# Gating weight loads, shortening the lag between two layers, and moving transposes to DMA in an attention + two-layer kernel

## The chip, the cores and the metric

One core of one Trainium2 chip. The metric is device microseconds of one execution, as the median of several; a "profile" is one traced execution, and its span is about 1.8 us shorter than the timed value of the same execution. Every ratio below is the mean time of one kernel's fast runs over the mean of the kernel before's fast runs in the same rounds, so it is not quite the ratio of the medians that are quoted beside it. Chips differ by about a per cent, so kernels are compared on one chip, or by these ratios. A run more than 1.5% above the fastest of its kernel is called slow and left out of the ratios; the medians quoted are of all runs.

## The reference

Eight batches; each has eight heads of 512 rows `x` and 32 rows `state`, 64 wide. Both attend to each other, and all rows go through a two-layer block.

```python
scores  = x @ state.T / 8 ;  a  = softmax(scores)  ; xread = a  @ state      # 512 rows a batch
scores2 = state @ x.T / 8 ;  a2 = softmax(scores2) ; sread = a2 @ x          # 32 rows a batch
rows = concat([xread, sread])           # heads side by side: (8 * 544) x 512
h = rows @ w_in                         # 512 -> 2048
g = s * relu(h) ** 2 + b
out = g @ w_out                         # 2048 -> 512, float32
```

## The kernel before

It folds `state @ w_in` into a matrix M for each batch, so that layer 1 of the 512 x rows is `a @ M`. Work is cut into slots. Batch `s` has 16 slots; slot `f` computes one 128-row block of the hidden layer, `h_f` (two matmuls of 512 columns), its relu on ScalarE and its square on VectorE, then a piece of the attention of a later batch (`todo`), then one "layer-2 slot" (four matmuls of 512 columns) of hidden blocks computed `LAG` slots earlier. I call the 16 slots of batch 0 "stage 0", those of batch 1 "stage 1", and so on. The order on TensorE is the program's; the other engines are ordered by a scheduler.

```python
# loads: x[0] and the first states on the hardware queues, all else from gpsimd, at once
nc.scalar.dma_start(stf[:, 0:NG, :], st_v[:, 0:NG, :])
nc.scalar.dma_start(ident16, ident_dr.ap())
for i in range(4):
    nc.sync.dma_start(xf[:, 2 * i : 2 * i + 2], x0_v[:, 2 * i : 2 * i + 2])
# ... cut: constants, casts of x[0] and state to fp16 ...
load_wi(0); load_wi(1); load_x(1); load_wi(2); load_wi(3)     # 512 KB fp16 each, cast from 1 MB fp32
for q in range(4): load_wo(q)
load_x(2)  # ... cut: the remaining states, x[3] to x[7] ...

def att_xT(b, i):             # transposes of x on TensorE, through PSUM
    ps = att_ps([P, 4, 2, P], FP16, f"xTps_{b}_{i}")
    # ... 8 x mm(ps[...], xn[b][...], ident16, is_transpose=True), then one copy to SBUF ...

def att_aT(b):                # transposes of the normalised softmax, likewise
    # ...
    for g in range(NG):
        nc.vector.tensor_scalar(a2, a["E"][g], q1[:, g : g + 1], None, ALU.mult)
        for c in range(SCH):
            mm(ps[:, g, c, :], a2[:, P * c : P * c + P], ident16, is_transpose=True)
    nc.vector.tensor_copy(aT, ps)

# main loop (TensorE in program order)
LAG = 20
for slot in range(NKF * (B + 1)):
    s, f = divmod(slot, NKF)
    # mm1_x(s, f): h_f of batch s; in stage 0 every third relu runs on VectorE
    # todo: pieces of batch s+1 (state and x transposes, T, D, M, aT, V)
    if slot >= LAG:
        mm2_slot(slot - LAG)  # batch 0: two row blocks by turns; later batches: one after the other
```

The softmax here doesn't subtract the row's maximum and nothing guards it: scores larger than these inputs give would overflow.

## Time and profile before

| | before |
|---|---|
| time, median | 258.82 us at first, 259.69 us with a fourth run |
| span of the profiled run | 256.8 us |
| `h_0` of batch 0 starts | 21.87 us |
| `h_0` of batch 1 starts (stage 1) | 43.62 us |
| layer 2 starts | 47.37 us |
| one batch afterwards | 25.57 us |

The page's view in 40 slices of 6.4 us gives busy shares in tenths, the granted TensorE clock in tenths, and the mean share of the 16 DMA engines.

```profile
PE   8189759997999999999999999999999999999970
DVE  1128968777468745874587458745874444433220
PEclk9679986999999999999999999999999999999998
DMA  7999999901111111111111111111101211121111
```

From about 60 us (in the tenth slice) on, TensorE is full at full clock; before that, and above all in the first 50 us, in which DMA is saturated, it is not. The chain of waits (start us, length us, what; some pieces of the view) says why:

```profile
2.25 10.92 DMA xf<-in_x_dram
...
22.03 0.45 PE h_0_302 L66 x2
...
29.42 1.24 DVE M_253 L276 x2
...
36.10 0.61 DVE M_253 L276
36.72 0.05 issue
36.76 1.03 PE h_12_525 L66 x2
```

The chain starts with the load of x[0] (`xf`), then, inside stage 0, runs over VectorE work. The timeline (start, length, engine, line, operation, idle time before it and what ended it) shows the last two pieces of x[0] cast, and `h_0` of two batches in the later stage:

```profile
10.95 0.48 DVE L116 CAST xn_115<-xf 128x512 f16<-128x512 f32 x1 [6.71 <-DMA xf<-in_x_dram]
13.19 0.62 ACT L116 CAST xn_115<-xf 128x512 f16<-128x512 f32 x1 [7.68 <-DMA xf<-in_x_dram]
...
94.79 0.38 PE L66 MATMUL h_0_1364<-a_3_0_1128,M_1141 128*128 128x512 f16 x1
...
120.36 0.38 PE L66 MATMUL h_0_1725<-a_4_0_1489,M_1502 128*128 128x512 f16 x1
```

The period is 120.36 - 94.79 = 25.57 us. The table of stretches for stage 0 of the kernel before follows, its columns named in its first line. Its DMA share is the time of all packets that start in the stretch over the time of 16 engines; packets overlap, so it can pass 1:

```profile
core 0: us, PE busy (x) PEld busy (x) DVE busy (x) ACT busy (x) POOL busy (x), PEclk, DMA share, GB/s
21.87:43.62 21.75, 17.40 (x190) 6.85 (x188) 18.00 (x41) 11.44 (x26) 4.37 (x5) 0.84 1.48 196
```

### The profile page before, as it was taken

Reading aid. Unit: us, or ns where it says so; the run is one execution under the profiler, and the core shown is the slowest. Engines: PE = TensorE matmul, PEld = TensorE weight load, DVE = VectorE, ACT = ScalarE, POOL = GpSimd, SP = SyncE. Lnnn points to the kernel's source line nnn. Section 1 sums busy time; section 2 is a strip of 40 time slices with the busy share of each in tenths; the row PEclk is TensorE's granted clock in tenths of the full one; section 3 lists DMA queues with packets and bytes.
Section 4 is the critical chain, followed back from the end, with each engine's and each line's share of the span. In section 5 each row is a group of like instructions: output and inputs, shape, how many; then the busy total and the mean of one; then the engine's idle time right before and its main releaser. Section 6 shows DMA issues by size and latency. Waiting matters only on the chain.

```text
span 256.8 us, 4444 instructions
## 1 busy us (share of the span) xinstructions
PE 235.6 (92%) x1772; PEld 108.9 (42%) x1772; DVE 146.6 (57%) x327; ACT 118.1 (46%) x255; POOL 15.0 (6%) x23
## 2 busy tenths in 40 slices
PE   8189759997999999999999999999999999999970
PEld 3034214442543454445434544454344444555430
DVE  1128968777468745874587458745874444433220
ACT  2074564862457445743574357435743444222000
POOL 6524210000000000000000000000000000000000
PEclk9679986999999999999999999999999999999998
DMA  7999999901111111111111111111101211121111
GB/s 169 198 195 207 203 181 198 139 0 41 43 41 41 43 41 43 41 41 46 41 43 41 43 41 44 40 41 43 52 31 46 79 42 41 43 82 41 50 52 65
DMA packets 21709, 18.71 MB, mean 73 GB/s; under 512 B 5048, under 2 KB 17336, under 8 KB 21688
## 3 DMA queue, kind: packets, MB, share of 16 engines
q0 software_dynamic: 14608, 8.26, 22.9%
q1 hardware_dynamic: 6664, 10.06, 11.3%
q8 instruction: 14, 0.23, 0.4%
q10 hardware_dynamic: 416, 0.10, 0.2%
q14 instruction: 7, 0.06, 0.1%
HBM read 17.76 MB, written 8.91 MB: 104 GB/s over the span
## 4 chain that ended last, share of the span: by engine, by line
PE 83%; DVE 6%; DMA 4%; ACT 2%; issue 1%; SPq 1%
DMA xf<-in_x_dram 4%; PE o_2_2011 L66 1%; PE o_3_974 L66 1%; PE o_2_2372 L66 1%; PE o_1_1921 L66 1%; PE o_2_2733 L66 1%; PE o_2_1650 L66 1%; PE o_2_1289 L66 1%; PE o_1_1199 L66 1%; PE o_0_728 L66 1%; PE o_1_2643 L66 1%; PE o_1_2282 L66 1%; PE o_1_1560 L66 1%; PE o_3_2109 L66 1%; PE o_3_1748 L66 1%; PE o_0_2554 L66 1%
## 5 line engine op out<-in xcount | busy, mean ns | idle before, releaser
L66 PE MATMUL warm_ps<-warm 128*128 128x512 f16 x26 | 9.9, 521 | 7.1 <-DVE stT_171 L196 5.2
L66 PEld LDWEIGHTS <-warm 128*128 128x128 f16 x26 | 3.0, 124 | 10.6 <-issue 9.0
L116 DVE CAST xn_115<-xf 128x512 f16<-128x512 f32 x2 | 0.9, 452 | 9.2 <-DMA xf<-in_x_dram 9.2
L116 ACT CAST xn_115<-xf 128x512 f16<-128x512 f32 x2 | 1.2, 618 | 9.5 <-DMA xf<-in_x_dram 9.5
L66 PEld LDWEIGHTS <-M_253 128*128 128x128 f16 x32 | 2.6, 103 | 6.0 <-DVE M_253 L276 3.5
L66 PEld LDWEIGHTS <-M_1502 128*128 128x128 f16 x32 | 3.1, 98 | 3.8
L66 PEld LDWEIGHTS <-M_760 128*128 128x128 f16 x32 | 3.1, 98 | 3.8
L66 PEld LDWEIGHTS <-M_1863 128*128 128x128 f16 x32 | 3.1, 98 | 3.8
L66 PEld LDWEIGHTS <-M_2224 128*128 128x128 f16 x32 | 3.1, 98 | 3.8
L66 PEld LDWEIGHTS <-M_2585 128*128 128x128 f16 x32 | 3.1, 98 | 3.8
L66 PEld LDWEIGHTS <-M_1141 128*128 128x128 f16 x32 | 3.1, 98 | 3.8
L66 PEld LDWEIGHTS <-M_493 128*128 128x128 f16 x32 | 2.9, 98 | 3.1 <-issue 0.2
L66 PEld LDWEIGHTS <-stT_171 64*32 64x32 f16 x48 | 1.1, 89 | 5.1 <-issue 4.9
L66 PEld LDWEIGHTS <-xn_115 128*64 128x64 f16 (+1 forms) x48 | 2.0, 115 | 1.8 <-issue 1.0
L340 ACT ACTIVATE r_11_898<-h_11_895 128x512 f16<-128x512 f32 x1 | 0.6, 597 | 4.5 <-PE h_11_895 L66 4.5
L66 PEld LDWEIGHTS <-st_114 128*128 128x128 f16 x16 | 1.6, 102 | 2.2 <-POOL st_114 L123 0.4
L66 PEld LDWEIGHTS <-bones_91 128*128 128x128 f16 x16 | 1.5, 98 | 2.1 <-issue 0.6
L66 PE MATMUL bias_ps<-wsum,ones_105 128*128 128x512 f32 x2 | 1.1, 644 | 1.4 <-DVE wsum L391 1.4
L361 DVE SCALAR_TENSOR_TENSOR osb_sr_3261<-o_sr_3244,s_bc,bias_bc 128x512 f32<-128x512 f32 x1 | 0.8, 751 | 2.7 <-PE o_sr_3244 L66 2.7
L361 DVE SCALAR_TENSOR_TENSOR osb_sr_3281<-o_sr_3264,s_bc,bias_bc 128x512 f32<-128x512 f32 x1 | 0.8, 751 | 2.7 <-PE o_sr_3264 L66 2.7
L361 DVE SCALAR_TENSOR_TENSOR osb_3_3241<-o_3_3224,s_bc,bias_bc 128x512 f32<-128x512 f32 x1 | 0.8, 750 | 2.7 <-PE o_3_3224 L66 2.7
L66 PEld LDWEIGHTS <-stT_312 64*32 64x32 f16 x48 | 0.7, 94 | 3.7 <-issue 3.7
(1753 smaller groups left out, 768.1 us busy)
## 6 DMA issues: line engine op xcount, KB each, us to landing
xf<-in_x_dram SPq DMA_DIRECT2D x4, 256.0 KB, 9.2
wi_124<-in_moe_w_in_dram POOLq DMA_DIRECT2D x1, 512.0 KB, 8.9
wi_126<-in_moe_w_in_dram POOLq DMA_DIRECT2D x1, 512.0 KB, 11.7
xn_128<-in_x_dram POOLq DMA_DIRECT2D x1, 512.0 KB, 12.4
wi_130<-in_moe_w_in_dram POOLq DMA_DIRECT2D x1, 512.0 KB, 14.0
wi_132<-in_moe_w_in_dram POOLq DMA_DIRECT2D x1, 512.0 KB, 15.8
wo_134<-in_moe_w_out_dram POOLq DMA_DIRECT2D x1, 512.0 KB, 17.7
wo_136<-in_moe_w_out_dram POOLq DMA_DIRECT2D x1, 512.0 KB, 20.5
```

The costliest lines, as they stand in the source:

```text
L66: return nc.tensor.matmul(out, lhsT, rhs, start=start, stop=stop, tile_position=tp, is_transpose=is_transpose, skip_group_check=True,)
L116: eng(xn[0][:, 2 * i : 2 * i + 2].rearrange("p h c d -> p h (c d)"), xf[:, 2 * i : 2 * i + 2],)
L340: nc.scalar.activation(r16, hps, AF.Relu)
L361: nc.vector.scalar_tensor_tensor(osb, ops, s_bc, bias_bc, ALU.mult, ALU.add)
```

## The change

Its intent is to use the first 50 us better and to take work off TensorE afterwards. Five parts:

1. gpsimd copies two columns of the identity before its first load, so the weight loads wait until the identity has landed and x[0] goes first ("the gate"). The cast of the first states moves from gpsimd to VectorE, so that it does not stand behind these loads.
2. Layer 2 runs 11 slots behind layer 1 instead of 20, so it starts inside stage 0. For that, all batches take two row blocks by turns. (One block after the other cannot be built at this lag: its fourth layer-2 slot would need hidden blocks that do not exist yet.)
3. x and state of batches 3 to 7 and the softmax of every batch are transposed by DMA on the sync queue, not by TensorE.
4. In stage 0, relus move from VectorE to ScalarE, and so do three copies of M.
5. V of a batch moves a stage later (V(0) and V(1) into stage 1).

```diff
+    nc.scalar.dma_start(ident16, ident_dr.ap())
     nc.scalar.dma_start(stf[:, 0:NG, :], st_v[:, 0:NG, :])
-    nc.scalar.dma_start(ident16, ident_dr.ap())
@@ loads
+    with tc.manual_schedule(engines={mybir.EngineType.Pool}):
+        gate = konst.tile([P, 2], FP16, name="gate")
+        nc.gpsimd.tensor_copy(gate, ident16[:, 0:2])
+        load_wi(0); load_wi(1); load_x(1); load_wi(2); load_wi(3)
+        load_wo(0); load_wo(1)          # cut: state casts of batches 1, 2
+        load_wo(2); load_x(2); load_wo(3)
@@ transposes
+    def dma_stT():
+        nc.sync.dma_start_transpose(stTd, st16[:, NB_HW * NG :].rearrange("p n k d -> p (n k d)"))
+    def dma_xT(b):
+        nc.sync.dma_start_transpose(xT.rearrange("p h k q -> p (h k) q"), xn[b].rearrange("p h c d -> p (h c d)"))
@@ att_aT
-            for c in range(SCH):
-                mm(ps[:, g, c, :], a2[:, P * c : P * c + P], ident16, is_transpose=True)
-        nc.vector.tensor_copy(aT, ps)
+            nc.sync.dma_start_transpose(aT[:, g], a2)
@@ att_M
-            if g == 1 and c % 2 == 1:
+            if g == 1 and (c % 2 == 1 or b < 2):
                 nc.scalar.copy(dst, ps[g])
@@ layer 2 and main loop
-        rr, part = divmod(f, 4)       # cut: batch 0 was by turns already
+        rr, part = 2 * (f // 8) + f % 2, f % 8 // 2
-        LAG = 20
+        LAG = 11
-                mm1_x(s, f, dve_relu=(s == 0 and f % 3 == 1))
+                mm1_x(s, f)
# cut: the table of pieces by slot, rewritten; fewer warm-up matmuls
```

More of the change, by code (lines that the diff above doesn't have):

```diff
@@ L85 @@
     st_v = state.rearrange("b (g hf) j d -> (hf j) (b g) d", g=NG)
-    stf = konst.tile([P, 2 * NG, D], FP32, name="stf")
+    NB_HW = 3
+    stf = konst.tile([P, NB_HW * NG, D], FP32, name="stf")
     xf = konst.tile([P, H, SCH * D], FP32, name="xf")
     x0_v = x[0].rearrange("h (q c) d -> q h (c d)", q=P)
+    nc.scalar.dma_start(ident16, ident_dr.ap())
     nc.scalar.dma_start(stf[:, 0:NG, :], st_v[:, 0:NG, :])
-    nc.scalar.dma_start(ident16, ident_dr.ap())
     for i in range(4):
@@ L94 @@
     nc.sync.dma_start(bones16, bones_dr.ap())
-    nc.sync.dma_start(stf[:, NG : 2 * NG, :], st_v[:, NG : 2 * NG, :])
+    nc.sync.dma_start(stf[:, NG:, :], st_v[:, NG : NB_HW * NG, :])
     ones16 = konst.tile([P, Ns], FP16, name="ones16")
@@ L123, in cast_st @@
             eng.tensor_copy(st16[:, b * NG : b * NG + NG, k, :], stf[:, b * NG : b * NG + NG])
-    cast_st(nc.gpsimd, 0)
+    cast_st(nc.vector, 0)
     cast_x0(nc.vector.tensor_copy, 0)
@@ L129 @@
     cast_x0(nc.scalar.copy, 3)
-    cast_st(nc.vector, 1)
     def load_x(b):
@@ L158, in load_wo @@
         wo.append(t)
-    load_wi(0)
-    load_wi(1)
-    load_x(1)
-    load_wi(2)
-    load_wi(3)
-    for q in range(4):
-        load_wo(q)
-    load_x(2)
-    for k in range(2):
-        nc.gpsimd.dma_start(out=st16[:, 2 * NG :, k, :], in_=st_v[:, 2 * NG :, :])
-    for b in range(3, B):
-        load_x(b)
+    with tc.manual_schedule(engines={mybir.EngineType.Pool}):
+        gate = konst.tile([P, 2], FP16, name="gate")
+        nc.gpsimd.tensor_copy(gate, ident16[:, 0:2])
+        load_wi(0)
+        load_wi(1)
+        load_x(1)
+        load_wi(2)
+        load_wi(3)
+        load_wo(0)
+        load_wo(1)
+        for b in range(1, NB_HW):
+            cast_st(nc.gpsimd, b)
+        load_wo(2)
+        load_x(2)
+        load_wo(3)
+        for k in range(2):
+            nc.gpsimd.dma_start(out=st16[:, NB_HW * NG :, k, :], in_=st_v[:, NB_HW * NG :, :])
+        for b in range(3, B):
+            load_x(b)
     def wof(f):
@@ L184 @@
     A = {}
+    stTd = konst.tile([P, (B - NB_HW) * NG, P], FP16, name="stTd")
+    def dma_stT():
+        nc.sync.dma_start_transpose(
+            stTd, st16[:, NB_HW * NG :].rearrange("p n k d -> p (n k d)")
+        )
+    def dma_xT(b):
+        xT = apool.tile([P, H, 2, P], FP16, name=f"xT_{b}", tag="xT")
+        nc.sync.dma_start_transpose(
+            xT.rearrange("p h k q -> p (h k) q"), xn[b].rearrange("p h c d -> p (h c d)")
+        )
+        A[b] = {
+            "stT": stTd[:, (b - NB_HW) * NG : (b - NB_HW + 1) * NG],
+            "xT": [xT[:, 0:4], xT[:, 4:8]],
+            "E": [],
+            "rs": [],
+            "a4": [],
+        }
     def att_stT(b):
@@ L279, in att_aT @@
         a = A[b]
-        ps = att_ps([P, NG, SCH, P], FP16, f"aTps_{b}")
+        aT = apool.tile([P, NG, SCH, P], FP16, name=f"aT_{b}", tag="aT")
         q1 = apool.tile([P, NG], FP32, name=f"q_{b}", tag="q")
@@ L284, in att_aT @@
         for g in range(NG):
-            a2 = apool.tile([P, S], FP16, name=f"a2_{b}_{g}", tag=f"a2{g}", bufs=1)
+            a2 = apool.tile([P, S], FP16, name=f"a2_{b}_{g}", tag=f"a2{g}")
             nc.vector.tensor_scalar(a2, a["E"][g], q1[:, g : g + 1], None, ALU.mult)
-            for c in range(SCH):
-                mm(ps[:, g, c, :], a2[:, P * c : P * c + P], ident16, is_transpose=True)
-        aT = apool.tile([P, NG, SCH, P], FP16, name=f"aT_{b}", tag="aT")
-        nc.vector.tensor_copy(aT, ps)
+            nc.sync.dma_start_transpose(aT[:, g], a2)
         a["aT"] = aT
@@ L310, in att_V, with pieces @@
         nc.vector.tensor_copy(srdT[:, :, b * Ns : (b + 1) * Ns], ps)
-    def pieces(b):
-        return [
-            (0, lambda: att_stT(b)),
-            (0, lambda: att_xT(b, 0)),
-            (1, lambda: att_xT(b, 1)),
-            (3, lambda: att_T(b)),
-            (5, lambda: att_D(b, 0)),
-            (6, lambda: att_M(b, 0)),
-            (7, lambda: att_D(b, 1)),
-            (8, lambda: att_M(b, 1)),
-            (9, lambda: att_aT(b)),
-            (10, lambda: att_M(b, 2)),
-            (12, lambda: att_M(b, 3)),
-            (13, lambda: att_V(b)),
-        ]
+    def pieces(s):
+        b = s + 1
+        todo = []
+        if b < B:
+            if b < NB_HW:
+                t0 = 4 if s else 3
+                todo += [
+                    (0, lambda: att_stT(b)),
+                    (t0, lambda: att_xT(b, 0)),
+                    (t0 + 1, lambda: att_xT(b, 1)),
+                ]
+            else:
+                t0 = -1
+            t0 += 2
+            todo += [
+                (t0, lambda: att_T(b)),
+                (t0 + 2, lambda: att_D(b, 0)),
+                (t0 + 3, lambda: att_D(b, 1)),
+                (t0 + 3, lambda: att_M(b, 0)),
+                (t0 + 4, lambda: att_aT(b)),
+                (t0 + 5, lambda: att_M(b, 1)),
+                (t0 + 7, lambda: att_M(b, 2)),
+                (t0 + 9, lambda: att_M(b, 3)),
+            ]
+        if s == 0:
+            todo += [(6, lambda: att_M(0, 2)), (9, lambda: att_M(0, 3))]
+        if s == 1:
+            todo += [(3, dma_stT), (12, lambda: att_V(0))]
+        if 0 < s < B:
+            todo += [(13, lambda: att_V(s))]
+        if NB_HW <= s + 2 < B:
+            todo += [(5 if s == 1 else 0, lambda: dma_xT(s + 2))]
+        return todo
     G = {}
@@ L415, in mm2_slot @@
         s, f = divmod(u, NKF)
-        rr, part = divmod(f, 4)
-        if s == 0:
-            rr, part = 2 * (f // 8) + f % 2, f % 8 // 2
-            if f == 6:
-                bias()
+        rr, part = 2 * (f // 8) + f % 2, f % 8 // 2
+        if u == 6:
+            bias()
         mm2_part(s, rr, 4 * part, 4 * part + 4, x_dst(s, rr))
@@ L426 @@
         att_stT(0)
-        warm_up(3)
-        att_xT(0, 0)
-        warm_up(3)
-        att_xT(0, 1)
-        warm_up(3)
-        att_T(0)
-        warm_up(4)
+        warm_up(2)
+        att_xT(0, 0)
+        warm_up(2)
+        att_xT(0, 1)
+        warm_up(2)
+        att_T(0)
+        warm_up(3)
         att_D(0, 0)
         att_D(0, 1)
+        warm_up(2)
         att_M(0, 0)
         warm_up(2)
+        att_M(0, 1)
         att_aT(0)
-        att_M(0, 1)
-        warm_up(2)
-        first = {
-            0: [lambda: att_stT(1)],
-            3: [lambda: att_xT(1, 0)],
-            4: [lambda: att_xT(1, 1)],
-            6: [lambda: att_T(1)],
-            5: [lambda: att_V(0)],
-            7: [lambda: att_M(0, 2)],
-            8: [lambda: att_D(1, 0)],
-            9: [lambda: att_D(1, 1)],
-            10: [lambda: att_M(1, 0)],
-            11: [lambda: att_M(0, 3)],
-            12: [lambda: att_M(1, 1)],
-            13: [lambda: att_M(1, 2), lambda: att_aT(1)],
-            14: [lambda: att_M(1, 3)],
-            15: [lambda: att_V(1)],
-        }
-        LAG = 20
+        LAG = 11
         for slot in range(NKF * (B + 1)):
@@ L460 @@
             if s < B:
-                mm1_x(s, f, dve_relu=(s == 0 and f % 3 == 1))
+                mm1_x(s, f)
             else:
                 mm1_sr(f)
-            if s == 0:
-                todo = first.get(f, [])
-            else:
-                todo = [fn for at, fn in pieces(s + 1) if at == f] if s + 1 < B else []
-            for fn in todo:
-                fn()
-            if slot >= LAG:
+            for at, fn in pieces(s):
+                if at == f:
+                    fn()
+            if LAG <= slot < LAG + NKF * B:
                 mm2_slot(slot - LAG)
-        for u in range(NKF * (B + 1) - LAG, NKF * B):
+        for u in range(min(NKF * (B + 1) - LAG, NKF * B), NKF * B):
             mm2_slot(u)
```

## The prediction

> **What bounds the kernel now.** Two stages. By the stretch-by-stretch table of busy time, TensorE is 100% busy at full clock from 60 us to about 249 us: the tensor-bound stage. One batch takes 25.57 us there (first-row-block output groups start at 76.47 and 102.04 in the chain of waits). Before 60 us it is not bound by work. The timeline shows why: the last two of four x[0] pieces (issued by 2.7 us) are cast only at 10.95 and 13.19, because the gpsimd weight loads run at once beside them; the first layer-1 matmul h_0 starts at 21.87. Then batch 0's sixteen slots last until 43, with VectorE busy 4.97 of 5 us in 25:30 and TensorE waiting on M copies (1.6 us for h_12), clock 0.6 to 0.7 for 35:45. Layer 2 begins only at 47.4. DMA runs saturated until about 51. From these durations I count about 29 us of TensorE work finished by 60 us: 31 us are lost.
>
> **What the change does.**
> 1. Gate: weights wait for the identity's arrival, about 3 us, so most of x[0] goes ahead of them. I expect x[0] complete by 7 to 9 us instead of 13, and h_0 at about 16 (8.2 us chain as before; it also needs the second w_in block, about 15).
> 2. Slot stage 0: VectorE loses 5 relus (0.68 each), 3 M copies (0.69), the aT copies (0.69 each) and V(0), V(1): about 20.6 to 14 us. ScalarE rises from about 13 to 18 us (16 relus at 0.6, 6 M copies at 0.6, exps and logs 4.8). So it becomes the limit: about 19 us, stage 1 starting at about 35 instead of 43.6.
> 3. Lag 11 puts 5 layer-2 slots (0.86 each) under that ScalarE-bound stage, where TensorE has room. It needs w_out by about 28 to 37; the last w_out block, now behind x[2], should land near 37 (33.4 before): about 1 us stall at the bias.
> 4. DMA transposes remove 64 + 90 TensorE transposes at 54 ns (8 take 0.44 us) = 8.3 us on the critical path, and their copies, which aren't critical. Price: 512 KB per x transpose. The Trainium skill, "DMA: Bandwidth & Descriptors", section "Latency and other measured facts", gives 261 GB/s for transposes, hence about 2 us each plus fixed cost, an estimate; no run shows it yet. The lead is over 12 slots, 18 us, and DMA is only 10 to 14% busy after 60 us. Hidden.
> 5. Two row blocks by turns: only about one slot to evict (0.75 us) before the bank is wanted. Batch 0 already runs so at 60:80 with TensorE 100% busy. No cost expected.
>
> **Sum.** From stage 1 on: layer 1 48.3, layer 2 123 x 0.863 = 106.1, state rows 13.9, bias 3.4 (57.3 to 60.7 now), attention 6 x 3.43 + 2.4 = 23.0: 194.7 us. 35 + 1 + 194.7 + tail 7.7 (PE end to span end) = 238.4, plus 1.9 between span and time: 240 us. Range 232 to 248. Chances: faster by over 2% 0.91, within 0.06, slower 0.03.
>
> **What would show it.** Both late x[0] casts before 9.5; h_0 at 15 to 18; ScalarE near 90% busy in stage 0; stage 1 (second h_0) at 33 to 38; batch period 24.1 us with TensorE 100% busy; x transposes landing within 10 us of issue; no TensorE wait on output evictions over 0.3 us.
>
> **What would make it wrong.** The gpsimd loads, once open, still crowd out the last x[0] piece (they took about four fifths of the rate before): h_0 near 20. w_out landing after 40. Transposes so slow (over 1 us per 128x128 block, 24 blocks a batch) that the sync queue, which also carries the outputs, backs up and V or T waits: then no gain. Psum turns stalling 0.5 us per pair: 8 us.

## The result

| | before | changed |
|---|---|---|
| time, median | 259.69 us | 241.55 us (240.56 to 242.95) |
| ratio, 95% interval | | 0.9312 (0.9236 to 0.9388) |
| span of the profiled run | 256.8 us | 239.8 us |
| `h_0` of batch 0 | 21.87 us | 15.46 us |
| `h_0` of batch 1 | 43.62 us | 37.75 us |
| layer 2 starts | 47.37 us | 30.82 us |
| one batch afterwards | 25.57 us | 24.13 us |

The same lines of the page of the changed kernel (slices of 6.0 us):

```profile
PE   7857898999999999999999999999999999999960
DVE  2354764658567735773586458645864535342520
PEclk9997999999999999999999999999999999999996
DMA  6999999999955013501380204020402012020211
```

TensorE is nearly full from the fifth slice (24 us) on. The DMA engines stay saturated until about 66 us instead of 51 (the last load lands at 61, and the outputs that had waited follow), and are far from idle afterwards. The start of the chain of waits:

```profile
0.74 2.48 DMA ident_90<-ident_const
3.22 0.05 issue
3.27 0.18 POOL gate L163
3.45 0.82 POOL wi_126 L144
4.28 0.73 POOL wi_128 L144
5.00 14.71 DMA xn_130<-in_x_dram
19.72 0.05 issue
19.76 0.77 PE xTps_0_331 L66 x8
```

x[0] is gone from the chain. What stands there now is the gate itself, and behind it x[1] (`xn_130`), issued at 5.00 and landed 14.71 us later. The timeline and the list of waits show this from both sides; the last line is the transpose of x[1], at slot 3 of stage 0.

```profile
5.75 0.43 DVE L117 CAST xn_115<-xf 128x512 f16<-128x512 f32 x1 [0.33 <-DMA xf<-in_x_dram]
6.55 0.62 ACT L117 CAST xn_115<-xf 128x512 f16<-128x512 f32 x1 [1.07 <-DMA xf<-in_x_dram]
...
15.46 0.39 PE L66 MATMUL h_0_298<-a_0_0_247,M_260 128*128 128x512 f16 x1
...
19.76 0.77 PE L66 MATMUL xTps_0_331<-ident_90,xn_130 128*128 128x128 f16 x8 [2.29 <-DMA xn_130<-in_x_dram]
```

```profile
PE xTps_0_331 L66 <- DMA xn_130<-in_x_dram: 2.3, 1, 2.3
PE Mps_1_0_276 L66 <- DMA wi_128<-in_moe_w_in_dram: 1.6, 1, 1.6
```

This list gives the total wait, the number of times and the longest. It covers the whole execution down to waits of 0.2 us, and it holds no wait of TensorE on an output eviction: the two row blocks by turns cost nothing that can be seen. The table of stretches for stage 0, and for the 3 us after that wait (columns as above):

```profile
15.46:37.75 22.29, 19.18 (x144) 7.58 (x137) 13.41 (x32) 15.59 (x35) 6.13 (x8) 0.92 1.32 195
...
20.00:23.00 3.00, 3.00 (x19) 1.64 (x16) 1.75 (x4) 0.60 (x1) 0.95 (x1) 0.52 1.23 197
```

VectorE fell from 18.00 to 13.41 us, as meant, yet stage 0 still lasts 22.29 us (21.75 before), now with five layer-2 slots in it. After the wait for x[1] the clock is at half, 0.52. The Trainium skill, "TensorE: Matmul & The Clock Gate", Part 1, says that the array falls back to half clock after an idle window of about 3.4 us; here the fall is seen after gaps of 1.6 and 2.3 us, so no idle time of that length was needed, and the cost of a wait was larger than the wait. In the later stage:

```profile
90.51 0.38 PE L66 MATMUL h_0_1322<-a_3_0_1073,M_1095 128*128 128x512 f16 x1
...
114.64 0.38 PE L66 MATMUL h_0_1650<-a_4_0_1401,M_1423 128*128 128x512 f16 x1
```

The period is 24.13 us, 1.44 us less: 26 transposes at about 55 ns. From `h_0` of batch 1 to the last matmul (ends 232.0) pass 194.25 us, then 7.8 us to the end of the span.

### The profile page after: what moved, and what is told of

Same layout as the page of the kernel before. It is cut to its first block, busy times and chain, and to the rows that moved or that the text cites. A ratio compares the mean times of both kernels' runs of the same rounds, so it can differ in the third digit from the quotient of the medians.

```text
span 239.8 us, 4165 instructions
## 1 busy us (share of the span) xinstructions
PE 223.5 (93%) x1614; PEld 99.1 (41%) x1614; DVE 129.0 (54%) x295; ACT 122.9 (51%) x264; POOL 15.4 (6%) x26
## 4 chain that ended last, share of the span: by engine, by line
PE 86%; DMA 7%; DVE 1%; ACT 1%; POOL 1%; issue 0%
DMA xn_130<-in_x_dram 6%; PE o_3_2092 L66 2%; PE o_3_1764 L66 2%; PE o_3_1108 L66 2%; PE o_0_852 L66 2%; PE o_3_2418 L66 2%; PE o_3_1436 L66 2%; PE o_0_1894 L66 2%; PE o_0_1566 L66 2%; PE o_0_1238 L66 2%; PE o_1_533 L66 2%; PE o_0_2222 L66 2%; PE o_0_2548 L66 1%; PE o_1_898 L66 1%; PE o_3_679 L66 1%; PE o_2_656 L66 1%
## 5 line engine op out<-in xcount | busy, mean ns | idle before, releaser
L66 PE MATMUL warm_ps<-warm 128*128 128x512 f16 x22 | 8.2, 503 | 1.2 <-DVE warm L79 1.2
L66 PEld LDWEIGHTS <-stTd 64*32 64x32 f16 x240 | 3.0, 89 | 10.6 <-issue 10.6
L66 PEld LDWEIGHTS <-M_1423 128*128 128x128 f16 x32 | 3.1, 98 | 3.8
L66 PEld LDWEIGHTS <-M_2079 128*128 128x128 f16 x32 | 3.1, 98 | 3.8
L66 PEld LDWEIGHTS <-M_1095 128*128 128x128 f16 x32 | 3.1, 98 | 3.8
L66 PEld LDWEIGHTS <-M_441 128*128 128x128 f16 x32 | 3.1, 98 | 3.8
L66 PEld LDWEIGHTS <-M_1751 128*128 128x128 f16 x32 | 3.1, 98 | 3.8
L66 PEld LDWEIGHTS <-M_789 128*128 128x128 f16 x32 | 3.1, 98 | 3.8
L66 PEld LDWEIGHTS <-M_2405 128*128 128x128 f16 x32 | 3.1, 98 | 3.8
L66 PEld LDWEIGHTS <-M_260 128*128 128x128 f16 x32 | 2.7, 104 | 3.5 <-issue 1.5
L66 PEld LDWEIGHTS <-warm 128*128 128x128 f16 x22 | 2.3, 120 | 4.4 <-issue 3.0
L66 PEld LDWEIGHTS <-stT_179 64*32 64x32 f16 x48 | 1.0, 89 | 6.3 <-issue 3.1
L66 PE MATMUL xTps_0_331<-ident_90,xn_130 128*128 128x128 f16 x8 | 0.8, 250 | 2.3 <-DMA xn_130<-in_x_dram 2.3
L66 PEld LDWEIGHTS <-bones_91 128*128 128x128 f16 x16 | 1.6, 97 | 2.2 <-issue 0.6
L384 ACT ACTIVATE r_2_637<-h_2_634 128x512 f16<-128x512 f32 x1 | 0.6, 597 | 3.6 <-PE h_2_634 L66 3.6
L177 POOL DMA_DIRECT2D st_114<-in_state_dram x2 | 1.9, 946 | 6.3 <-DMA xn_130<-in_x_dram 3.9
L384 ACT ACTIVATE r_4_345<-h_4_342 128x512 f16<-128x512 f32 x1 | 0.6, 597 | 3.2 <-PE h_4_342 L66 3.2
L405 DVE SCALAR_TENSOR_TENSOR osb_sr_3077<-o_sr_3060,s_bc,bias_bc 128x512 f32<-128x512 f32 x1 | 0.8, 751 | 2.7 <-PE o_sr_3060 L66 2.7
L405 DVE SCALAR_TENSOR_TENSOR osb_sr_3097<-o_sr_3080,s_bc,bias_bc 128x512 f32<-128x512 f32 x1 | 0.8, 751 | 2.7 <-PE o_sr_3080 L66 2.7
```

The lines of the kernel that those rows point to most:

```text
L66: return nc.tensor.matmul(out, lhsT, rhs, start=start, stop=stop, tile_position=tp, is_transpose=is_transpose, skip_group_check=True,)
L177: nc.gpsimd.dma_start(out=st16[:, NB_HW * NG :, k, :], in_=st_v[:, NB_HW * NG :, :])
L384: nc.scalar.activation(r16, hps, AF.Relu)
L405: nc.vector.scalar_tensor_tensor(osb, ops, s_bc, bias_bc, ALU.mult, ALU.add)
```

## The experiments

The total was as forecast, so the questions were which parts earn it, whether the gate's 6 us are real although it stands at the head of the new chain, and why stage 0 did not shrink. My theory: batch 0's DMA transposes (two of 128 KB, issued at 11.95 and 13.33 us, in the saturated stretch) push x[1] back, and that swallows what the gate wins. The rival: x[1] is late only because it stands behind the gate and two weight blocks.

As a common mark I use the first state transpose of batch 2 on TensorE, 0.43 us after `h_0` of batch 1 ("the mark"): 44.06 before, 38.18 changed. Everything up to it is the first stage's doing. One profile's mark varies: 38.18 and 39.19 in two profiles of the same changed kernel. The runs were made in three groups, each on one chip; the kernel before was timed in each. In the second group five of its eleven runs were slow (above 260.36 us).

### e1_no_gate: the changed kernel without the gate

```diff
-        nc.gpsimd.tensor_copy(gate, ident16[:, 0:2])
+        nc.gpsimd.memset(gate, 0.0)
```

> The changed kernel with the weight loads not waiting for the identity. Theory A (the gate is worth part of what it moves, because it also delays x[1], which in the changed kernel's trace holds TensorE 2.3 us at 19.76): the last x[0] cast goes back to about 13 us, h_0 to about 21, but x[1] is there by 17 and stage 0 shrinks from 22.3 to 19 to 20 us: second h_0 near 41 instead of 37.75, time about 244.5, ratio to before near 0.943. Rival B (the gate is worth all of the 6.4 us by which h_0 moved): about 248, ratio 0.957. Rival C (worth nothing): 241.5.

Measured: 242.26 us, ratio 0.9388 (0.9319 to 0.9457); mark 38.21. The interval overlaps that of the changed kernel (0.9312 and, later, 0.9341). x[0] was late again, as this timeline of e1 shows, and `h_0` came at 18.85, not 15.46, but x[1] was there in time and stage 0 took 18.9 us:

```profile
9.52 0.43 DVE L117 CAST xn<-xf 128x512 f16<-128x512 f32 x1 [4.13 <-DMA xf<-in_x_dram]
11.73 0.62 ACT L117 CAST xn<-xf 128x512 f16<-128x512 f32 x1 [6.35 <-DMA xf<-in_x_dram]
```

So in the changed kernel the gate moves `h_0` by 3.4 us and, in this pair of profiles, hands it all back by slot 7, which starts at 25.4 us in both. B (0.957) falls. Between A (0.943) and C the interval does not decide: it holds both, and by the ratios the gate is worth 0.5 to 0.8% here, which is not resolved from nothing.

### e2_gate_only: the kernel before with the gate alone

```diff
+    nc.scalar.dma_start(ident16, ident_dr.ap())
     nc.scalar.dma_start(stf[:, 0:NG, :], st_v[:, 0:NG, :])
-    nc.scalar.dma_start(ident16, ident_dr.ap())
-    cast_st(nc.gpsimd, 0)
+    cast_st(nc.vector, 0)
+    gate = konst.tile([P, 2], FP16, name="gate")
+    nc.gpsimd.tensor_copy(gate, ident16[:, 0:2])     # ahead of the loads, which keep their order
```

> The kernel before with the gate alone (identity first, first state cast on VectorE). Theory A: h_0 moves from 21.87 to about 15.5 to 16, but x[1] lands near 19 and stage 0 stays VectorE-bound at about 21.75 us plus 1 to 2 of waiting: second h_0 near 39 instead of 43.6, time about 254.5, ratio 0.982. Rival B: all of the 6.4 us is kept: 252.5, ratio 0.975. Rival C: nothing is kept, ratio 1.0.

Measured: 252.86 us against 258.69, ratio 0.9782 (0.9726 to 0.9838); `h_0` at 15.30, mark 38.01 instead of 44.06. By the mark, nearly the whole 6.4 us are kept (B), by the medians 5.8 us; the interval holds both A and B, not C. Here the gate is worth 2.2% (1.6 to 2.7%): this kernel transposes on TensorE, and x[1] is not held up by it. The same part is worth 2.2% in one kernel and 0.5 to 0.8%, not resolved from nothing, in the other.

### e3_pe_transposes: the changed kernel with all transposes on TensorE

```diff
-            nc.sync.dma_start_transpose(aT[:, g], a2)
+            for c in range(SCH):
+                mm(ps[:, g, c, :], a2[:, P * c : P * c + P], ident16, is_transpose=True)
+        nc.vector.tensor_copy(aT, ps)
-            if b < NB_HW:                  # x and state: by TensorE for the first batches only
+            if b < B:
# cut: dma_stT and dma_xT are no longer called
```

> The changed kernel with all transposes on TensorE again (x, state and softmax of every batch), the schedule otherwise kept. Theory: each full batch costs 26 x 54 ns = 1.4 us more on TensorE, so the period is near 25.5 us instead of 24.1; total +8.3, less up to 1.5 to 2 us because no transposes by DMA disturb x[1] in the saturated stretch: time about 248, ratio 0.956. Rival (TensorE transposes hide under other work, or their PSUM copies push VectorE over): below 243.5 or above 252.

Measured: 247.11 us, ratio 0.9529 (0.9451 to 0.9606), one of its four runs slow; period 25.47 us (state transposes at 89.28 and 114.75), mark 34.72. As expected: 1.3 to 1.4 us a batch lost later, and 3.5 us won before the mark, more than the 1.5 to 2 that I had given. The DMA transposes are a net gain of about 2%, but they cost something in the first stage.

### e4_lag20: the changed kernel with the old lag

```diff
-        LAG = 11
+        LAG = 20
```

> The changed kernel with layer 2 again 20 slots behind. On record: 5 layer-2 slots of 0.86 us hidden in stage 0, so without them +4.3 us (246, ratio 0.949). Refined by the trace of the changed kernel, whose chain of waits runs over TensorE from 29.2 us to the end of stage 0: stage 0 would shrink by about 2.5 us without them, so the loss is only about 1.8 us (243.5, ratio 0.938), and the second h_0 comes near 35 instead of 37.75.

Measured: 243.16 us, ratio 0.9407 (0.9351 to 0.9463), mark 34.59. Against 0.9312 and 0.9341 this is 0.7 to 1.0% or 1.7 to 2.5 us, the refined figure and not the 4.3 us on record: stage 0 without the five layer-2 slots was 3.6 us shorter. They were not laid into idle time; most of their time came straight out of a stage that TensorE filled at its end. The intervals of e4 and of the changed kernel overlap, so what is shown is that the worth of the shorter lag is small, not its exact size.

### r_after_again, e6_pe_aT0, e7_x1_first, e8_both: what delays stage 0

The changed kernel once more:

> The changed kernel unaltered, for comparison on the same chip: ratio to before near 0.931 to 0.938, second h_0 at 37.8, x[1] landing near 19.7.

Measured: 241.61 us, ratio 0.9341 (0.9276 to 0.9406), mark 39.19. TensorE waited until 21.16 us for x[1] in this profile, later still than the expected 19.7, and its clock was at half twice, from 15.1 us and from 21.9 us, for 3.4 us each.

e6 takes batch 0's two softmax transposes back to TensorE, ahead of the second weight product, where they fit while it waits for weights:

```diff
-            nc.sync.dma_start_transpose(aT[:, g], a2)
+            if b == 0:
+                for c in range(SCH):
+                    mm(ps[:, g, c, :], a2[:, P * c : P * c + P], ident16, is_transpose=True)
+            else:
+                nc.sync.dma_start_transpose(aT[:, g], a2)     # cut: PSUM tile and its copy, if b == 0
-        att_M(0, 1)
         att_aT(0)
+        att_M(0, 1)
```

> The changed kernel with only batch 0's softmax transposes (2 x 128 KB) on TensorE, while it waits for weights anyway. Theory (DMA transposes in the saturated stretch push x[1] back): x[1] lands about 1.5 us earlier, near 18.2, second h_0 near 36 instead of 37.75, about 1.7 us less than the changed kernel (ratio to it 0.993). Rival (x[1] is late only because it stands behind the gate and two weight blocks): x[1] still near 19.7 and the time that of the changed kernel.

Measured: 238.49 us, ratio 0.9220 (0.9168 to 0.9272), mark 33.82: 3.1 us less than the changed kernel on the same chip, nearly twice what the theory had given. When the second weight block and x[1] landed can be read from gpsimd, two of whose later loads wait for them. The changed kernel first, then e6:

```profile
15.36 0.75 POOL L154 DMA_DIRECT2D wo_148<-in_moe_w_out_dram  x1 [1.66 <-DMA wi_128<-in_moe_w_in_dram]
20.00 0.95 POOL L177 DMA_DIRECT2D st_114<-in_state_dram  x1 [3.88 <-DMA xn_130<-in_x_dram]
```

```profile
13.69 0.75 POOL L154 DMA_DIRECT2D wo<-in_moe_w_out_dram  x1 [1.69 <-DMA wi<-in_moe_w_in_dram]
16.33 0.95 POOL L177 DMA_DIRECT2D st<-in_state_dram  x1 [1.88 <-DMA xn<-in_x_dram]
```

In e6 x[1] came 3.7 us earlier and the second weight block 1.7 us. Only the difference, 2.0 us, can be laid to the transposes. The first weight block was 1.7 us earlier too (gpsimd's load that waits for it issues at 11.12 instead of 12.81), and the packets that the trace keeps, by time, queue and size, show that no packet of the two transposes (1024 of 256 bytes) ran before 16.0 us, though they were issued at 11.95 and 13.33. What moved these 1.7 us is not shown. For the 2.0 us there is more than one pair of profiles: from the second weight block to x[1], by the same gpsimd loads, pass 4.6, 6.0 and 5.6 us in the three profiles with the gate, this order of loads and these transposes on DMA (changed, r_after_again, e4), and 2.6 us in all five with them on TensorE (e3, e6, e6_again, e10, e11). The packets say how: from 16 to 20 us, beside the transposes, the loads of gpsimd moved 153 GB/s in the changed kernel and 203 in e6, and 96 of the 1024 packets of x[1] still had to start then; in e6 all had started by 15.7.

TensorE then waits for no load before the bias, and keeps its clock. Stage 0 of e6 (columns as above):

```profile
14.59:33.39 18.80, 17.60 (x144) 7.07 (x138) 13.75 (x33) 15.59 (x35) 5.39 (x6) 1.00 1.28 201
```

18.80 us instead of 22.29 with the same work: ScalarE's 15.59 us are equal in both, and TensorE's 17.60 instead of 19.18 us are about what the half clock had cost. This is the length that the prediction had expected, but with TensorE, at 17.60 us, more the limit than ScalarE.

e7 keeps the DMA transposes and loads x[1] ahead of the second weight block:

```diff
-        load_wi(1)
         load_x(1)
+        load_wi(1)
+            todo += [(3, lambda: att_M(0, 1))]      # was in the preamble
```

> The changed kernel with x[1] loaded ahead of the second w_in block, whose product moves from the preamble to slot 3. Theory (stage 0 is held up by what must land before slot 4, one load at a time): x[1] lands near 17, h_0 comes at 14.5, the second w_in block lands near 19.5 but is wanted only before h_4; second h_0 near 36, 1.5 to 2.5 us less. Rival: the last of the three loads lands when it did, so slot 4 starts at 20 to 21 as before and nothing is gained.

Measured: 239.61 us, ratio 0.9262 (0.9214 to 0.9311), mark 35.59; x[1] was transposed at 15.86 without a wait, and the weight block was waited for at 17.63. 2.0 us less than the changed kernel, as the theory had it. So order matters too. The packets agree with e6: here all of x[1] had started by 14.3 us, before the first packet of a transpose (16.3), and the weight block, wanted later, took the delay. The rival is right about that part of it.

> Both of the two edits above. Theory: the gains add in part, second h_0 near 34.5, but the last w_out block then lands (38 to 39) after it is wanted at the bias, so the total falls by 2 to 3 us and not by the whole 3.3. Rival: no gain over the better of the two alone.

e8 has the edits of e6 and e7 together. Measured: 239.20 us, ratio 0.9251 (0.9201 to 0.9300), mark 35.96. No gain over the better of the two alone: the rival holds. With x[1] early, TensorE waits 1.1 us at slot 3 for the second weight block, which e6 gets in time, besides 1.2 us for the first; the gains do not add. My reason for it was not the one: the list of waits has none on w_out.

### e6_again, e9_e6_no_gate, e10_e6_wo3_first, e11_e6_pe_aT1: the gate once x[1] is early, and what is left

> The kernel of e6_pe_aT0 once more, for comparison on the same chip: ratio to before near 0.922, second h_0 near 34, no wait of TensorE on a load before the bias.

Measured: 238.27 us, ratio 0.9237 (0.9188 to 0.9286), mark 33.83. One of its six runs (241.34 us) was slow. One small miss: TensorE waited 0.5 us for the second weight block and 0.3 us for x[1] in this profile.

> e6 without the gate. Theory (the gate's gain was real but swallowed by the late x[1], which batch 0's DMA transposes had pushed back): now that x[1] is early, losing the gate shows: h_0 near 18.5 to 19 instead of 14.6, stage 0 still 18.8 us, second h_0 near 37.5, time 3 us or more above e6. Rival (the gate is worth nothing in any case): the time of e6.

The edit is that of e1, on e6. Measured: 241.66 us, ratio 0.9375 (0.9328 to 0.9421), mark 40.28 in a profile that was its slowest run. The gate is worth 3.4 us here by the medians, as the theory said, where beside the DMA transposes of batch 0 its worth could not be resolved. `h_0` came at 20.91, later than expected.

| | transposes of batch 0's softmax by DMA | by TensorE |
|---|---|---|
| without gate | 0.9388 (e1) | 0.9375 (e9) |
| with gate | 0.9312, 0.9341 (changed) | 0.9220, 0.9237 (e6) |

Read by columns the gate is worth 0.5 to 0.8% on the left, which the intervals do not resolve, and 1.4 to 1.6% on the right; read by rows, taking the transposes off DMA does nothing where x[0] is what stage 0 waits for, and 0.8 to 1.2% where it is x[1]. That each part takes full effect only if the other stretch is not the later one is what the traces show (late x[0] in e1 and e9, late x[1] in the changed kernel); by the times alone the difference between the columns, about 0.8%, is of the size of the intervals.

> e6 with the last w_out block loaded ahead of x[2]. Theory: the only wait on a load that e6 has left, 0.45 us at the bias, goes: 0.3 to 0.6 us less than e6. Rival: x[2] is then late for its TensorE transposes at slot 4 of stage 1 and the time is that of e6 or more.

```diff
-        load_x(2)
         load_wo(3)
+        load_x(2)
```

Measured: 237.73 us, ratio 0.9228 (0.9181 to 0.9275), on the same chip as e6_again's 0.9237. The wait at the bias is gone from the list, and the medians differ by 0.5 us, but the intervals do not tell the two apart: inconclusive. e6 and e10 are the fastest versions here, both ahead of the changed kernel.

> e6 with batch 1's softmax transposes on TensorE too. Theory: they fall where nothing waits for a load any more but w_out, so taking them off the DMA queues saves at most the 0.45 us at the bias and costs 0.43 us of TensorE: within 0.5 us of e6. Rival (every DMA transpose in the saturated stretch costs time as batch 0's did): 2 to 3 us less than e6.

The edit is that of e6 with `b < 2`. Measured: 238.72 us, ratio 0.9260 (0.9220 to 0.9299): not faster than e6, within 0.5 us of it. In e6 batch 1's transposes are issued in the saturated stretch as well, from 23.05 us on, but they cost nothing that can be seen. The rival falls: not every DMA transpose there costs time; batch 0's did, where x[1] stood behind them on the chain.

## Why the prediction was right, point by point

The measured 241.55 us lies 1.6 us above the forecast 240, well within the range. Its sum, term by term:

| term | predicted | measured |
|---|---|---|
| start of stage 1 | 35 | 37.75 |
| stage 1 to the last matmul | 1 + 194.7 | 194.25 |
| tail of the span | 7.7 | 7.8 |
| span to time | 1.9 | 1.8 |

- **The steady stage** was right. "batch period 24.1 us with TensorE 100% busy" was measured as 24.13, and e3 shows that it is the transposes: with them the period is 25.47.
- **Two row blocks by turns**: "No cost expected" was right; TensorE waits for no eviction. Batch 0 of the kernel before had already shown it.
- **The gate moves x[0]**: "Both late x[0] casts before 9.5; h_0 at 15 to 18" was right, 5.75 and 6.55, and 15.46. That `h_0` "also needs the second w_in block, about 15" was right as well: it landed at 15.1 and was the last thing waited for.
- **The step that was mis-sized** is step 2, "about 19 us, stage 1 starting at about 35". Stage 0 took 22.3 us. Of that, about 3.5 us is the late x[1] with the half clock after it: with batch 0's transposes off the DMA queues the same stage took 18.8 us (19.1 in e6_again, against 23.0 in r_after_again). The reason, "So it becomes the limit" of ScalarE, did not hold: ScalarE was busy 15.59 of 22.29 us, 70% and not "near 90%". Its busy time was over-counted too (18 us), because its operations overlap a little: relus of 0.60 us start 0.49 us apart (16.65 and 17.14). That e6's stage 0 takes 18.8 us, nearly the forecast 19, is luck: the limit was another.
- **The step behind that** is step 4: "Hidden." I had looked at where the transposed data is wanted and at the mean DMA load after 60 us, and not at the transposes that the change issues before 60 us, where DMA is saturated. The data itself was hidden; its traffic was not. e6 is 3.1 us faster for two transposes, though not all of it need be theirs, as said there.
- **Lag 11**: "where TensorE has room" was too hopeful. e4 puts its worth at about 2 us (not sharply, as said there) and not the 4.3 that five slots take. The stall at the bias was 0.8 us, near the forecast "about 1 us", but it was for VectorE's sum of w_out; the last w_out block landed at 39.7, not "near 37".
- **The x transposes** land "within 10 us of issue" only in the quiet stage (4.3, 4.4 and 6.1 us); the first took 16.8 us. The sync queue was held 8.0 and 8.3 us by the issue of each of the first two, so that the first finished output, evicted at 43.6, was issued only at 60.93. This cost nothing that TensorE waited for. The timeline of the sync queue:

```profile
44.43 8.00 SPq L202 DMA_TRANSPOSE xT_702<-xn_152  x1
52.52 8.32 SPq L202 DMA_TRANSPOSE xT_1001<-xn_154  x1
60.93 0.53 SPq L406 DMA_DIRECT2D out_dram<-osb_0_631  x1
```

The errors offset each other in part: stage 1 started 2.75 us later than forecast, and from there to the last matmul it took 1.45 us less, so the sum stayed within 1.6 us. That closeness is partly luck; a right total did not prove the parts.

What a DMA transpose takes can be read from the quiet stage. In the stretch from 116 to 124 us both kernels write two outputs of 256 KB; the changed one (first) also transposes most of 768 KB, e3 (second) none:

```profile
116.00:124.00 8.00, 8.00 (x59) 3.26 (x57) 6.31 (x16) 6.46 (x17) 0.00 (x0) 1.00 0.76 150
```

```profile
116.00:124.00 8.00, 8.00 (x65) 3.95 (x64) 4.65 (x10) 3.26 (x6) 0.00 (x0) 1.00 0.18 67
```

The DMA share rises from 0.18 to 0.76, which is 0.58 x 8 us = 4.6 us of 16 engines for (150 - 67) x 8 = 0.66 MB, about 145 GB/s; the outputs took 0.18 x 8 = 1.4 us for 0.52 MB, about 360 GB/s. The same working for 92 to 101 us, where 0.77 MB are transposed (shares 0.62 and 0.17), gives about 190. By this estimate, 145 to 190 GB/s, the two 128 KB transposes of batch 0 need 1.4 to 1.8 us of the engines. That is a little less than the 2.0 us by which x[1] fell behind. Why their packets start only at 16.0 us, 4 us after the issue (in the quiet stage 1.2 us after it: issued at 92.89, first packet at 94.06), was not tested, and stays open.

## What to carry to other kernels

When work is moved to DMA, look at what the DMA queues carry from the moment of issue on and at who waits next for a load, not only at when the moved result is wanted; early transposes may belong on TensorE even if all later ones belong on DMA. When two waits end close together, removing one gives only the difference to the other, so test a part in both settings before it is called useful or useless. Filling a stage with another layer's work pays only for the idle time that the stage really has.

## What the Trainium skill lacked or had wrong

- "Advanced Engine Details and Errata", section "X-Bar Transpose (TRN2)", says that transposes by DMA are as fast as regular DMAs, and "DMA: Bandwidth & Descriptors", section "Latency and other measured facts", gives 261 GB/s, 350 to 400 if contiguous. Here, SBUF to SBUF, they moved about 145 to 190 GB/s by the engines' busy share, an estimate, beside about 360 for plain output writes.
- "DMA: Bandwidth & Descriptors" has no figure for a transpose beside saturated loads: two of 128 KB there took 8.4 and 10.4 us to land instead of 2.4 to 3.9, the loads beside them fell from 203 to 153 GB/s, and x[1] came 4.6 to 6.0 us after the second weight block instead of 2.6.
- The same page lets the issuing engine's time be "usually small relative to the DMA itself" (section "Issuing engines are not separate DMA queues"). A 512 KB transpose held the sync queue for 1.3 to 2.0 us in the quiet stage and for 8.0 and 8.3 us while loads saturated DMA, with all outputs queued behind it.
- "TensorE: Matmul & The Clock Gate" has no gaps over about 3.4 us as its rule; of short gaps that come often it tells too, but with no length. Here the granted clock fell to half at 20.09 us after gaps of 1.6 and 2.3 us that lay 2.4 us apart, and in e4 at 13.66 us, before which, TensorE's first 1.19 us aside, no gap was longer than 1.1 us. In the 3.41 us before these falls TensorE was busy for 1.1 and 1.8 us, so it was not idle throughout.
